# Raw-x queries in columns for the first layer-two unit of a batch, the norm's squares on DVE, 78 halves kept, and a new order

## Chip, cores and metric

The kernel runs on one core of one Trainium2 chip. The time is device microseconds per execution. The kernel before has a median of 285.7 us over 3 runs, from 284.73 to 285.88 us.

## What is computed

Two layers of decode with batch 4 and one token per batch entry, both layers with the same weights and the same caches. Each is a layer norm, attention over a cache of 4096 keys with 8 key/value heads (4 query heads on each), a residual sum, a second layer norm, a gated unit and a residual sum:

```
x = x + _A_ref(_layernorm(x, axis=-1), A_k_cache, A_v_cache, A_wq, A_wo)
x = x + _B_ref(_layernorm(x, axis=-1), B_w_gate, B_w_up, B_w_down)
x = x + _A_ref(_layernorm(x, axis=-1), A_k_cache, A_v_cache, A_wq, A_wo)
x = x + _B_ref(_layernorm(x, axis=-1), B_w_gate, B_w_up, B_w_down)
```

The caches are 32 MB each, in bf16, and do not fit on the core. Since both layers read the same cache, what is still in SBUF when layer two needs it isn't read again.

## The kernel before, in words

**Units.** The attention is cut into 16 units, written as three digits: batch entry, group of four key/value heads, layer (0 is layer one). `UNITS` names their order. A unit has four heads; K and V of a head are two *halves* each, of 512 KB (2048 keys). SBUF has a ring of 28 slots of one half each. A load fetches one half, or a *pair* (both halves of a head, 1 MB, when two neighbouring slots are free). `LOADS` is the list of all loads in the order in which SP issues them, weights between them. What `LOADS` doesn't name for a layer-two unit is *kept* from layer one: its slot stays taken until then. Counted from that table, the kernel before loads 181 halves and keeps 75 of 256, in 67 pairs and 47 single halves.

**A unit's work.** `queries` (L730) forms the unit's query from x and wq, spreads it (L767) and scales it into `zq` (L778). For each K half that comes from a load DVE transposes it in place (L805), and PE multiplies it with `zq` into the scores S (L813). `unit_probs` takes the maximum (L837 to L844), the exponential on ACT (L851), transposes the probabilities (L857, L862, L872). `unit_values` multiplies them with V (L905), ACT copies the result into a slot just read (L935, or into `p_sb`, L927), PE merges the heads (L958), and in layer one `wo` is applied and added to x (L1005, L1017).

**The chain of a batch entry.** When both layer-one units of a batch entry are done, `chain` (L1159) runs its norm (`layer_norm`, L1025, and `rstd`, L1043), gate and up products (L1069), the gated product (L1101, L1110, L1120), the down product (L1138), the sum into x (L1174) and the second norm. Only then can a layer-two query of that entry be formed: 16 matmuls that give it as rows (L743), an ACT copy (L752), 4 matmuls that turn it into columns (L757), an ACT copy (L762), the spreading (L767) and, with the inverse deviation `rs2` in the mask (L773), `zq`. The query needs x with its mean taken off (L1031).

**What sets the order.** `_Plan.schedule` (L143) takes all instructions with costs and ranks (the numbers `SHIFTS`, `CHAIN` and the like) and writes one list for each engine, gives each load its slots, and puts filler matmuls (L1380) where PE would wait. Each engine then runs its list in order. SP waits before a load until the slot's last reader is done, and every load behind it waits too.

**End.** When the last V half has landed, the rest of the last unit, the last `wo` part, the fourth norm and gated unit and the result follow (`last_part`, `last_chain`).

## Time and profile before

| | |
|---|---|
| median of 3 runs | 285.7 us (284.73 to 285.88) |
| the profiled execution | 286.48 us, of it the span of the profile 284.5 us, 1.98 us around it |
| busy | PE 227.0 us, DVE 166.5, ACT 67.6, POOL 10.7 |
| DMA | 108.8 MB through SP's queue, 94.7% of 16 engines' span |
| SP's loads | 35 V and 32 K pairs, 24 V and 23 K halves, 9 weight loads |
| granted TensorE clock | 0.946 |

Line 2 of the page cuts the span into 40 slices of 7.1 us. In the timeline of SP a row is a run of loads, from the first issue to the end of the last; a gap between rows is SP waiting for a slot. In the chain of waits "SPq L611" is SP's sequencer at a load of K or V, and a DMA row runs from an issue to its landing.

### The profile page before, as it was taken

How to read it: one execution, taken by the hardware profiler on the slowest of the kernel's cores; microseconds unless marked ns; L12 is line 12 of the kernel's file. 1: busy time of each engine (PE TensorE's matmuls, PEld its weight loads, DVE VectorE, ACT ScalarE, POOL GpSimd, SP SyncE). 2: the span in 40 equal slices, each digit the busy share in tenths (PEclk: the TensorE clock that was granted, in tenths of full speed). 3: DMA queues.
4: the chain of work that ended last, by engine and by line, in shares of the span. 5: the costliest groups of instructions: out<-in, count | busy, mean ns of one | idle time of the engine just before them, and what ended most of it. 6: DMA issues, size and time to landing. Idle time of an engine off the chain costs nothing.

```text
span 284.5 us, 7805 instructions
## 1 busy us (share of the span) xinstructions
PE 227.0 (80%) x3426; PEld 113.9 (40%) x3426; DVE 166.5 (59%) x340; ACT 67.6 (24%) x179; POOL 10.7 (4%) x39
## 2 busy tenths in 40 slices
PE   1007675669899883999989999889988898888997
PEld 1003322224455431444553444435443343534664
DVE  4537773954112493877354998304599786578222
ACT  1001002001411320231533302324232103632511
POOL 6100000000000000000000000000000000000000
PEclk9999997599799998999995999988799999999999
DMA  7999999999999999999999999998999999999910
GB/s 275 425 424 422 409 409 394 422 384 411 409 427 384 311 380 424 420 416 415 415 409 415 413 412 419 420 408 316 403 407 423 422 416 412 414 403 426 406 47 3
DMA packets 21393, 109.30 MB, mean 384 GB/s; under 512 B 2032, under 2 KB 4080, under 8 KB 12144
## 3 DMA queue, kind: packets, MB, share of 16 engines
q1 hardware_dynamic: 21296, 108.80, 94.7%
q8 instruction: 27, 0.44, 0.6%
q14 instruction: 6, 0.05, 0.0%
q10 hardware_dynamic: 64, 0.01, 0.0%
HBM read 108.79 MB, written 0.00 MB: 382 GB/s over the span
## 4 chain that ended last, share of the span: by engine, by line
PE 39%; DMA 39%; SPq 11%; DVE 7%; issue 2%; ACT 1%; DVEq 0%; ACTq 0%
DMA slots<-in_A_v_cache_dram 20%; PE S_ps L813 14%; DMA slots<-in_A_k_cache_dram 11%; SPq L611 10%; DMA wo<-in_A_wo_dram 8%; PE O_ps L905 6%; PE PT_ps L1380 4%; DVE slots L805 4%; PE M_ps L1005 3%; PE Q_ps L743 2%; PE G_ps L1140 2%; PE M_ps L958 2%; PE G_ps L1069 1%; PE U_ps L1069 1%; SPq L620 1%
## 5 line engine op out<-in xcount | busy, mean ns | idle before, releaser
L805 DVE STREAM_TRANSPOSE slots<-slots 128x1024 int32<-128x1024 int32 x87 | 103.9, 1223 | 31.1 <-DMA slots<-in_A_k_cache_dram 30.5
L813 PE MATMUL S_ps<-slots,zq 128*32 128x512 bf16 x512 | 81.0, 444 | 15.5 <-DVE slots L805 10.7
L905 PE MATMUL O_ps<-slots,pt_sb 128*16 128x512 bf16 x504 | 40.9, 410 | 10.9 <-DMA slots<-in_A_v_cache_dram 8.1
L813 PEld LDWEIGHTS S_ps<-slots,zq 128*32 128x32 bf16 x512 | 25.4, 105 | 51.9 <-DVE slots L805 17.9
L1380 PE MATMUL PT_ps<-wq 128*128 128x512 bf16 (+1 forms) x148 | 38.4, 365 | 0.7 <-ACT pt_sb L872 0.7
L935 ACT ACTIVATE slots<-O_ps 128x512 bf16<-128x512 f32 (+1 forms) x24 | 14.3, 596 | 34.5 <-PE O_ps L905 34.3
L905 PEld LDWEIGHTS O_ps<-slots,pt_sb 128*16 128x16 bf16 x504 | 11.7, 90 | 23.6 <-DMA slots<-in_A_v_cache_dram 9.0
L1380 PEld LDWEIGHTS PT_ps<-wq 128*128 128x128 bf16 x148 | 12.4, 99 | 16.1 <-issue 6.2
L872 ACT ACTIVATE pt_sb<-PT_ps 128x256 bf16<-128x256 f32 x32 | 11.0, 382 | 32.0 <-PE PT_ps L862 21.7
L851 ACT ACTIVATE p_sb<-S_ps,pt_sb 128x512 bf16<-128x512 f32 x16 | 13.3, 832 | 18.8 <-DVE pt_sb L844 16.0
L1005 PEld LDWEIGHTS M_ps<-oT,wo 128*128 128x128 bf16 x512 | 14.5, 96 | 7.9 <-issue 3.0
L1005 PE MATMUL M_ps<-oT,wo 128*128 128x32 bf16 x512 | 16.5, 177 | 0.4 <-DVE oT L980 0.4
L837 DVE TENSOR_REDUCE small<-S_ps 128x1 f32<-128x512 f32 x16 | 10.9, 684 | 9.8 <-PE S_ps L813 9.1
L712 PE MATMUL Q_ps<-small,wq 128*128 128x4 bf16 x128 | 3.7, 166 | 14.2 <-DMA wq<-in_A_wq_dram 14.2
L1057 POOL TENSOR_TENSOR stat<-real,small 128x1 f32<-128x1 f32 x8 | 4.4, 551 | 235.3 <-ACT real L1053 235.3
L958 PE MATMUL M_ps<-small,slots 128*64 128x4 bf16 (+2 forms) x196 | 9.2, 176 | 2.3 <-ACT slots L935 1.9
L958 PEld LDWEIGHTS M_ps<-small,slots 128*128 128x128 bf16 (+1 forms) x196 | 6.8, 103 | 10.1 <-ACT slots L935 5.4
L743 PE MATMUL Q_ps<-wq,small 128*1 128x512 bf16 x128 | 10.3, 387 | 0.5 <-DVE small L1031 0.4
L773 ACT ACTIVATE real<-real,stat 128x4 f32<-128x4 f32 x16 | 4.4, 293 | 25.7 <-DVE zq L778 19.8
L984 DVE TENSOR_TENSOR oT<-M_ps,real 64x8 bf16<-64x8 f32 x32 | 5.1, 159 | 8.8 <-PE M_ps L958 8.3
L927 ACT ACTIVATE p_sb<-O_ps 128x512 bf16<-128x512 f32 x8 | 4.8, 597 | 21.5 <-PE O_ps L905 17.0
L712 PEld LDWEIGHTS Q_ps<-small,wq 128*128 128x128 bf16 x128 | 3.6, 104 | 15.1 <-issue 15.1
(123 smaller groups left out, 195.6 us busy)
## 6 DMA issues: line engine op xcount, KB each, us to landing
slots<-in_A_v_cache_dram SPq DMA_DIRECT2D x35, 1024.0 KB, 10.8
slots<-in_A_k_cache_dram SPq DMA_DIRECT2D x32, 1024.0 KB, 10.3
slots<-in_A_v_cache_dram SPq DMA_DIRECT2D x24, 512.0 KB, 11.4
slots<-in_A_k_cache_dram SPq DMA_DIRECT2D x23, 512.0 KB, 8.4
wq<-in_A_wq_dram SPq DMA_DIRECT2D x2, 2048.0 KB, 14.6
wo<-in_A_wo_dram SPq DMA_DIRECT2D x4, 1024.0 KB, 19.8
wg<-in_B_w_gate_dram SPq DMA_DIRECT2D x1, 1792.0 KB, 18.3
wu<-in_B_w_up_dram SPq DMA_DIRECT2D x1, 1792.0 KB, 22.2
```

The source lines that it names most:

```text
L611: return e.dma_start(o, src)
L743: fns.append(lambda e, k=k, s=s: e.matmul(Q_ps[32 * s:32 * s + 1, :], lhsT=xT[:, b, k:k + 1], rhs=wq[:, k, hg * HC + s * 512:hg * HC + (s ...
L805: "dve", lambda e, t=t: e.transpose(ring[t.slot].bitcast(dt.int32), ring[t.slot].bitcast(dt.int32)),
L813: fns.append(lambda e, s=s, t=t, nn=nn, q=q: e.matmul(S_ps[qi][32 * s:32 * s + 32, :], lhsT=window(qi, s * NQ + nn, q), rhs=ring[t.slot].r ...
L837: dve(lambda e: e.tensor_reduce(ml[at], bank, AX.X, ALU.max, negate=True), [f"S{qi}s{s}" for s in ss], keys("ml", ss), 0.7)
L851: lambda e: e.activation(p_sb[at].rearrange("p (t j r) -> p t r j", j=32, r=2), bank.rearrange("p (t r j) -> p t r j", r=2, j=32), ACTF.Ex ...
L872: "act", lambda e, pr=pr: e.activation(pt_sb[:, (2 * i + pr) % 3], PT_ps[:, 256 * pr:256 * pr + 256], ACTF.Copy),
L905: fns.append(lambda e, m=m, at=at, v=v, c=c, q=q, pt=pt, bank=bank, x0=x0, x1=x1: e.matmul(bank[m:m + 16, x0:x1], lhsT=pt[:, at:at + 16], ...
L935: lambda e, lent=lent, rows=rows, o_ps=o_ps, rows_of=rows_of, cols=cols: e.activation(ring[lent.slot][rows, 0:cols], rows_of(o_ps[rows, 0: ...
L958: return e.matmul(o, lhsT=turned[:, tt * P + at:tt * P + at + n], rhs=heads(tt), start=(tt == 0), stop=(tt == 3))
L1005: fns.append(lambda e, k=k, n=n, h0=h0: e.matmul(M_ps[:, k * WIDE:(k + 1) * WIDE], lhsT=wo[:, h0 + n, k * P:(k + 1) * P], rhs=oT[:, b, h0 ...
L1380: return lambda e: e.matmul(PT_ps[:, column:column + width], lhsT=wq[:, 0, 0:P], rhs=wq[:, 0, 0:width], start=True, stop=True)
```

## The change

It does five things.

1. **The first layer-two query of a batch entry as columns.** `queries` has a new case `soon` (the first layer-two unit of that entry in `UNITS`): 64 matmuls of 32 columns with a 128x128 piece of wq as weights (L811 of the new kernel) give the query in columns, with no copy and no turning. The other four layer-two queries keep the 16 matmuls (L823), the copy (L832) and the turning (L837).
2. **Raw x.** All layer-two queries are formed from x itself. Two new helpers, `column_sums(0)` and `(1)`, form the negative column sums of wq once (128 matmuls at L780, two DVE copies at L789); one DVE operation (L843) adds mean times column sum to the raw query in place of the ACT copy. `rs2` no longer scales the mask, but the maximum (one more DVE operation in `unit_probs`, L935) and the exponential (its scale). The sum after the down product is written twice, first as `xT` for the query, then as x (L1282).
3. **The first norm's squares.** `layer_norm` sums x squared on DVE (L1122) beside the matmul that sums x, and `rstd` takes four times the squared mean off it on DVE (L1136, L1140, L1155) in place of three ACT operations. The second norm keeps its ACT operations (L1294, L1296) with its copy of the mean now `mean_of`.
4. **The planner.** Fillers may also go into the bank G and begin at 30 us instead of 55 us, its model of the PE clock has four phases, and its model of the DMA has 16 lanes. `SCRATCH` goes from 256 to 64 bytes.
5. **The tables.** All of them are new: the units' order, `LOADS`, `GROUPS`, the places lent to the gated unit, the ranks. Counted from the new `LOADS`, 178 halves are loaded and 78 kept, in 46 pairs and 86 single halves (31 of these are half of a head that is stored as a pair). The weights are the same nine loads.

The units before, and the core of the diff:

```
-UNITS = "000 010 100 011 110 200 001 111 210 300 211 310 101 201 311 301"
```

```diff
+UNITS = "000 010 011 100 001 110 200 111 101 210 211 300 310 201 311 301"
...
-        bus = DMA_START
+        lanes = [DMA_START] * 16
...
+            while held_wq:
+                room = fill_room(t)
+                if room is None or room[0] > at:
+                    return
+                t, reader, bank = room
+                op = _Op(len(self.ops), "pe", [self.fill(bank, FILL)], 0.2, 0.0, "pe", 1)
+                op.pairs, op.columns = 1, 4 * FILL
...
+                for since in crossed[fetches:]:
+                    lane = (fetches - 1) % 16
+                    lanes[lane] = max(lanes[lane], since) + DMA_LAG
+                    fetches += 1
+                middle = 0.0
+                for a in lanes:
+                    middle += a / 16
+                begin = op.end + DMA_DELAY
+                late = min(1.0, max(0.0, (begin - middle) / DMA_LOW + 1.0)) if middle > 20.0 else 0.0
+                lanes = [max(a, begin) + (op.size / DMA_RATE + DMA_AGAIN * late) for a in lanes]
+                op.end = max(lanes) + DMA_END + DMA_SPREAD
...
-    SCRATCH = 256
+    SCRATCH = 64
...
+    def column_sums(hg):
+        S.stage = f"c{hg}"
+        r = max(place["wq0"], place["wq1"]) + 25.0
+        for c0 in range(0, HG, 4):
+            fns = []
+            for c in range(c0, c0 + 4):
+                for k in range(KD):
+                    fns.append(lambda e, c=c, k=k: e.matmul(
+                        Q_ps[:, c * WIDE:(c + 1) * WIDE], lhsT=wq[:, k, hg * HC + c * DH:hg * HC + (c + 1) * DH],
+                        rhs=minus.broadcast_to([P, WIDE]), start=(k == 0), stop=(k == KD - 1),
+                    ))
+            S.put(
+                "pe", fns, reads=["wq0", "wq1", "Qz", "minus"], writes=[own("Q", c0 == 0)], rank=r, columns=len(fns) * 4 * WIDE,
+                lock="Q" if c0 == 0 else None,
+            )
+        S.put(
+            "dve", lambda e: e.tensor_copy(col_sum[:, hg * HG:(hg + 1) * HG], Q_ps[:, bass.ds(0, HG, step=WIDE)]),
+            reads=[own("Q")], writes=[f"cs{hg}"], cost=0.2, rank=r, free="Q",
+        )
...
+            soon = not any(u[0] == b and u[2] == 1 for u in seq[:i])
+            if soon:
+                for c0 in range(0, HG, 4):
+                    fns = []
+                    for c in range(c0, c0 + 4):
+                        for k in range(KD):
+                            fns.append(lambda e, c=c, k=k: e.matmul(
+                                Q_ps[:, c * WIDE:(c + 1) * WIDE], lhsT=wq[:, k, hg * HC + c * DH:hg * HC + (c + 1) * DH],
+                                rhs=xT[:, b, k:k + 1].broadcast_to([P, WIDE]), start=(k == 0), stop=(k == KD - 1),
+                            ))
...
+            S.put(
+                "dve",
+                lambda e, soon=soon: e.scalar_tensor_tensor(
+                    out=q2, in0=col_sum[:, hg * HG:(hg + 1) * HG], scalar=mean_of[:, b:b + 1],
+                    in1=Q_ps[:, bass.ds(0, HG, step=WIDE if soon else 1)], op0=ALU.mult, op1=ALU.add,
+                ),
+                reads=[own("Q"), f"mn{b}", f"cs{hg}"], writes=["q2"], cost=0.2, rank=rank,
             )
...
+        by, by_key = mask, "mask"
+        if l == 0:
+            by, by_key = maskrs[:, qi], f"maskrs{qi}"
+            S.put(
+                "act", lambda e: e.activation(by, mask, ACTF.Copy, scale=rs),
+                reads=["mask", rs_key], writes=[by_key], cost=0.2, rank=rank,
+            )
...
+        rs, rs_key = 1.0, []
+        if l == 1:
+            rs, rs_key = rs2[at, b:b + 1], [f"rs2{b}"]
+            dve(
+                lambda e: e.tensor_scalar(nM[at], nM[at], rs, None, op0=ALU.mult),
+                keys("nM", ss) + rs_key, keys("nM", ss), 0.16,
+            )
...
+                ACTF.Exp, bias=tr[at, 0:1], scale=rs, accum_out=ls[at],
...
+            "dve", lambda e: e.scalar_tensor_tensor(
+                out=junk, in0=x[:, b], scalar=1.0, in1=x[:, b], op0=ALU.mult, op1=ALU.mult, accum_out=xsq[:, b:b + 1]
+            ),
+            reads=[f"x{b}"], writes=["junk", f"xsq{b}"], cost=0.25, rank=rank,
...
+            "dve", lambda e: e.tensor_scalar(less, U_ps[:, 0:1], U_ps[:, 0:1], 4.0, op0=ALU.mult, op1=ALU.mult),
+            reads=["U"], writes=["less"], cost=0.16, rank=rank,
+        )
+        S.put(
+            "dve", lambda e: e.tensor_scalar(less, less, -4.0 * eps, None, op0=ALU.add),
+            writes=["less"], cost=0.16, rank=rank,
...
+            S.put(
+                "dve", lambda e: e.tensor_scalar(var[:, b:b + 1], ps_tile[:, 16:17], less, least, op0=ALU.subtract, op1=ALU.max),
+                reads=[bank, "less"], writes=["junk"], cost=0.16, rank=rank, **then,
...
+        for o, o_keys, more in ((xT, [f"xT{b}"], {}), (x, [f"x{b}", f"xsum{b}"], dict(accum_out=xsum[:, b:b + 1]))):
+            S.put(
+                "dve",
+                lambda e, o=o, more=more: e.scalar_tensor_tensor(
+                    out=o[:, b], in0=G_ps[:, bass.ds(0, KD, step=WIDE)], scalar=rs, in1=x[:, b], op0=ALU.mult, op1=ALU.add, **more
+                ),
+                reads=["G", f"rsg{b}", f"x{b}"], writes=o_keys, cost=0.2, rank=rank,
...
+        mean = mean_of[:, b:b + 1]
+        S.put(
+            "pe", lambda e: e.matmul(U_ps[:, 0:1], lhsT=ones, rhs=xsum[:, b:b + 1], start=True, stop=True),
+            reads=[f"xsum{b}", "ones"], writes=["U"], cost=0.35, rank=rank, pairs=2,
+        )
+        S.put("act", lambda e: e.activation(mean, U_ps[:, 0:1], ACTF.Copy), reads=["U"], writes=[f"mn{b}"], cost=0.18, rank=rank)
+        S.put(
+            "act", lambda e: e.activation(junk, x[:, b], ACTF.Square, bias=mean, scale=-1.0, accum_out=xsq[:, b:b + 1]),
+            reads=[f"x{b}", f"mn{b}"], writes=["junk", f"xsq{b}"], cost=0.25, rank=rank + 1.0,
+        )
...
+            for h in range(2):
+                column_sums(h)
```

**The first chain on PE.** Here are PE's rows from behind the down product (L1140, 56 matmuls, the row just ahead of these) of batch entry 0 to the scores of its first layer-two unit (011, in both kernels): L1380 is a filler, L1027 and L1049 are the second norm's, L905 and L958 values and merge of unit 010, L743 the query in rows, L757 its turning, L767 the spreading, L813 the scores. Before:

```order
L1380 MATMUL PT_ps<-wq 128x512
L1027 MATMUL U_ps<-stat 128x1
L905 MATMUL O_ps<-slots,pt_sb 16x512 x4
L743 MATMUL Q_ps<-wq,small 1x512 x8
L1049 MATMUL U_ps<-stat 128x1
L743 MATMUL Q_ps<-wq,small 1x512 x8
L905 MATMUL O_ps<-slots,pt_sb 16x512 x8
L757 MATMUL Q_ps<-small,p_sb 128x4 x4
L905 MATMUL O_ps<-slots,pt_sb 16x512 x4
L767 MATMUL Q_ps<-small,ident 32x4x4 x16
L958 MATMUL M_ps<-small,slots 128x32 x4
L813 MATMUL S_ps<-slots,zq 32x512 x32
```

After (L1247 down product, L1502 a filler, L1291 and L1150 the second norm's, L811 the query in columns, L823 the next query in rows, L852 the spreading, L901 scores, first five of unit 100, then of 011 with the next ones):

```order
L1247 MATMUL G_ps<-slots,wd 128x32 x56
L1502 MATMUL PT_ps<-wq 128x512
L811 MATMUL Q_ps<-small,wq 128x32 x16
L1291 MATMUL U_ps<-stat 128x1
L811 MATMUL Q_ps<-small,wq 128x32 x32
L1150 MATMUL U_ps<-stat 128x1
L811 MATMUL Q_ps<-small,wq 128x32 x16
L901 MATMUL S_ps<-slots,zq 32x512 x5
L852 MATMUL Q_ps<-small,ident 32x4x4 x16
L901 MATMUL S_ps<-slots,zq 32x512 x35
L823 MATMUL Q_ps<-wq,small 1x512 x16
```

The turning and its copy are gone and no V product stands in the chain any more; the scores of unit 100's first K halves now stand behind the new columns.

**SP's loads behind the weights of the gated unit.** From `wd` on, with the semaphores each load waits for (128x2048 is a half, 128x4096 a pair). Before, three loads wait only for the values of unit 000 and the fourth (K, waiting for PE, DVE and ACT) for the down product that has its slot:

```order
L620 DMA wd<-in_B_w_down_dram 128x7168
L611 DMA slots<-in_A_v_cache_dram 128x4096 [waits sem_pe]
L611 DMA slots<-in_A_v_cache_dram 128x2048 [waits sem_pe]
L611 DMA slots<-in_A_v_cache_dram 128x2048 [waits sem_pe,sem_act]
L611 DMA slots<-in_A_k_cache_dram 128x2048 [waits sem_pe,sem_dve,sem_act]
L611 DMA slots<-in_A_k_cache_dram 128x2048 [waits sem_pe] x3
L611 DMA slots<-in_A_k_cache_dram 128x2048 [waits sem_pe,sem_act]
L611 DMA slots<-in_A_k_cache_dram 128x2048 [waits sem_pe]
L611 DMA slots<-in_A_v_cache_dram 128x4096 [waits sem_pe]
L611 DMA slots<-in_A_k_cache_dram 128x4096
L611 DMA slots<-in_A_v_cache_dram 128x4096
```

After, the five loads behind `wd` wait for values of units 000 and 010, the sixth (V, waiting for PE, DVE and ACT) for the down product, the two K halves behind it for the first scores of unit 100, the pairs behind those for the scores of 011:

```order
L665 DMA wd<-in_B_w_down_dram 128x7168
L656 DMA slots<-in_A_k_cache_dram 128x2048 [waits sem_pe]
L656 DMA slots<-in_A_k_cache_dram 128x2048 [waits sem_pe,sem_act]
L656 DMA slots<-in_A_k_cache_dram 128x2048 [waits sem_pe] x2
L656 DMA slots<-in_A_v_cache_dram 128x2048 [waits sem_pe,sem_act]
L656 DMA slots<-in_A_v_cache_dram 128x2048 [waits sem_pe,sem_dve,sem_act]
L656 DMA slots<-in_A_k_cache_dram 128x2048 [waits sem_pe,sem_dve] x2
L656 DMA slots<-in_A_k_cache_dram 128x4096 [waits sem_pe] x2
L656 DMA slots<-in_A_k_cache_dram 128x4096
L656 DMA slots<-in_A_k_cache_dram 128x2048 x2
```

What stands behind `wd` without a wait for the chain went from one pair and two halves to five halves.

**SP's loads around the fourth chain.** Before, from a V pair of the last layer-one unit (310) on: four K halves of unit 201, then V pairs of 101:

```order
L611 DMA slots<-in_A_v_cache_dram 128x4096 [waits sem_pe,sem_dve]
L611 DMA slots<-in_A_k_cache_dram 128x2048 [waits sem_pe,sem_dve] x4
L611 DMA slots<-in_A_v_cache_dram 128x4096 [waits sem_pe,sem_dve]
L611 DMA slots<-in_A_v_cache_dram 128x4096 [waits sem_pe]
L611 DMA slots<-in_A_v_cache_dram 128x4096 [waits sem_dve]
L611 DMA slots<-in_A_v_cache_dram 128x2048 [waits sem_pe,sem_dve]
L611 DMA slots<-in_A_v_cache_dram 128x2048 [waits sem_dve]
L611 DMA slots<-in_A_v_cache_dram 128x2048 [waits sem_pe,sem_dve]
L611 DMA slots<-in_A_k_cache_dram 128x2048 [waits sem_dve]
```

After, from the last V pair of 310 on: nine K halves of unit 201 and 301, then V halves and K halves in turn:

```order
L656 DMA slots<-in_A_v_cache_dram 128x4096 [waits sem_pe]
L656 DMA slots<-in_A_k_cache_dram 128x2048
L656 DMA slots<-in_A_k_cache_dram 128x2048 [waits sem_pe,sem_act]
L656 DMA slots<-in_A_k_cache_dram 128x2048 [waits sem_pe]
L656 DMA slots<-in_A_k_cache_dram 128x2048
L656 DMA slots<-in_A_k_cache_dram 128x2048 [waits sem_pe]
L656 DMA slots<-in_A_k_cache_dram 128x2048 [waits sem_pe,sem_act] x2
L656 DMA slots<-in_A_k_cache_dram 128x2048 [waits sem_pe,sem_dve]
L656 DMA slots<-in_A_k_cache_dram 128x2048
L656 DMA slots<-in_A_v_cache_dram 128x4096 [waits sem_pe,sem_dve]
L656 DMA slots<-in_A_v_cache_dram 128x2048 [waits sem_pe]
L656 DMA slots<-in_A_k_cache_dram 128x2048 [waits sem_dve]
```

In the new order PE's rows around this chain are (L901 scores of 201, L1100 the `wo` product that ends 310's values, L1128 the norm's sum, L1176 gate and up, L1247 the first 24 matmuls of down; L1150 the inverse deviation, L1502 fillers):

```order
L901 MATMUL S_ps<-slots,zq 32x512 x2
L1100 MATMUL M_ps<-oT,wo 128x32 x32
L901 MATMUL S_ps<-slots,zq 32x512 x6
L1128 MATMUL U_ps<-stat 128x1
L1502 MATMUL PT_ps<-wq 128x512 x5
L1176 MATMUL G_ps<-wg,small 1x448 x8
L1150 MATMUL M_ps<-stat 128x1
L1176 MATMUL G_ps<-wg,small 1x448 x8
L1176 MATMUL U_ps<-wu,small 1x448 x16
L901 MATMUL S_ps<-slots,zq 32x512 x14
L1247 MATMUL G_ps<-slots,wd 128x32 x24
L901 MATMUL S_ps<-slots,zq 32x512 x2
```

The eighth of the nine K halves (waiting for PE and DVE) takes the slot of 201's first K half, whose scores stand on both sides of the `wo` product.

221 lines of the change are left out of this document (118 added, 103 removed).

## Prediction

> **What bounds the kernel now.** I read the page first: part 2 for the DMA row, then part 3 for the queues.
>
> ```profile
> PE   1007675669899883999989999889988898888997
> DMA  7999999999999999999999999998999999999910
> GB/s 275 425 424 422 409 409 394 422 384 411 409 427 384 311 380 424 420 416 415 415 409 415 413 412 419 420 408 316 403 407 423 422 416 412 414 403 426 406 47 3
> q1 hardware_dynamic: 21296, 108.80, 94.7%
> q8 instruction: 27, 0.44, 0.6%
> ```
>
> The DMA digit is 9 from the second slice to the 38th but once: the loads bound this kernel, while PE has slices of 5 to 7. What counts is bytes, the rate at which they flow, and the slices in which the flow is thin: the 14th (311 GB/s) and the 28th (316). I then asked for stretches by window, to have the two thin ones beside full ones.
>
> ```profile
> core 0: us, PE busy (x) PEld busy (x) DVE busy (x) ACT busy (x) POOL busy (x), PEclk, DMA share, GB/s
> 7.00:24.00 17.00, 2.13 (x80) 1.98 (x80) 7.52 (x7) 0.93 (x3) 1.29 (x3) 1.00 1.01 425
> 88.00:104.00 16.00, 14.25 (x225) 7.38 (x225) 8.57 (x19) 4.01 (x13) 0.55 (x1) 1.00 0.92 339
> 141.00:151.00 10.00, 8.84 (x176) 5.01 (x168) 4.67 (x14) 4.41 (x14) 0.90 (x2) 0.91 1.03 411
> 188.00:202.00 14.00, 12.68 (x230) 6.68 (x234) 5.25 (x14) 5.01 (x17) 1.10 (x2) 0.82 0.95 364
> 206.00:226.00 20.00, 17.17 (x226) 7.80 (x224) 17.95 (x27) 5.58 (x14) 0.00 (x0) 1.00 1.01 417
> ```
>
> 88 to 104 moved 339 x 16 = 5.42 MB; at the 411 of a full stretch that takes 13.2 us, so **2.8 us** were lost. 188 to 202 moved 5.10 MB, 12.4 us at 411: **1.6** lost. Together 4.4 us of thin flow, and no third such place. Why it is thin the timeline of SP shows (start, length, loads in a run), with the landing times of the DMA view:
>
> ```profile
> 64.65 7.10 SPq L620 DMA_DIRECT2D wd<-in_B_w_down_dram  x1
> 71.80 4.88 SPq L611 DMA_DIRECT2D slots<-in_A_v_cache_dram  x3
> 91.42 6.39 SPq L611 DMA_DIRECT2D slots<-in_A_k_cache_dram  x6
> 98.41 0.33 SPq L611 DMA_DIRECT2D slots<-in_A_v_cache_dram  x1
> wd<-in_B_w_down_dram SPq DMA_DIRECT2D x1, 1792.0 KB, 24.7
> slots<-in_A_k_cache_dram SPq DMA_DIRECT2D x1, 512.0 KB, 4.1
> ```
>
> From 76.7 to 91.4 SP issues nothing. `wd` lands at 64.65 + 24.7 = 89.35, the down product follows, and at 91.42 the half that gets its slot is issued (the second row is that half: 4.1 us to land with an emptied queue). By then only a pair and two halves were queued behind `wd`. The chain of waits has the steps:
>
> ```profile
> 80.88 0.90 PE M_ps L1005 x32
> 89.94 1.41 PE G_ps L1140 x56
> 91.36 0.24 DVE real L1174 x2
> 91.65 0.38 PE U_ps L1027 x2
> 92.03 0.53 PE O_ps L905 x4
> 94.02 0.61 ACT p_sb L752
> 94.93 0.55 PE O_ps L905 x4
> 95.50 0.61 ACT slots L935
> 96.42 1.93 PE S_ps L813 x29
> ```
>
> The end follows from the last load:
>
> ```profile
> 255.44 18.38 DMA slots<-in_A_v_cache_dram
> 273.86 0.30 PE G_ps L905 x2
> 282.43 0.27 ACT oT L1342
> ```
>
> It lands at 273.82 and 10.7 us of tail follow to the span's 284.5. So the time is (bytes at the full rate) + (thin flow) + (tail) + what lies around the span. I work against the profiled 286.48 and carry the difference to the median of 285.7, 0.8 us lower.
>
> **Part 1: the loads.** The tables go from 181 halves to 178, in 46 pairs and 86 single halves instead of 67 and 47: 39 halves more and 21 pairs fewer. What flows from 141 to 151 was issued from 132.5 to 145, and is seven single halves behind a pair; what flows from 206 to 226 was issued from 202 to 218, and is nine pairs:
>
> ```profile
> slots<-in_A_v_cache_dram SPq DMA_DIRECT2D x5, 512.0 KB, 8.1
> slots<-in_A_v_cache_dram SPq DMA_DIRECT2D x1, 1024.0 KB, 10.1
> slots<-in_A_k_cache_dram SPq DMA_DIRECT2D x2, 512.0 KB, 10.2
> slots<-in_A_k_cache_dram SPq DMA_DIRECT2D x6, 1024.0 KB, 8.4
> slots<-in_A_v_cache_dram SPq DMA_DIRECT2D x3, 1024.0 KB, 10.6
> ```
>
> A half is 0.524 MB: 1.276 us at 411. A pair is 1.049 MB: 2.515 at 417, or 2.467 at the 425 of 7 to 24 us. 39 x 1.276 = 49.8; 21 pairs are 52.8 or 51.8. The change is -3.0 or -2.0; I take the middle, **-2.5**. So splitting costs next to nothing in a full queue. Instructions are loaded too: 27 packets for 7805 instructions in the rows above, one per 289. The new program has about 650 more (324 matmuls, each counted with its weight load): 2.3 packets more, 0.6% of 284.5 us over 27 is 0.06 us of all 16 engines each, 1 us for one engine if it takes them alone. I take **+0.2**.
>
> The Trainium skill, page "DMA: Bandwidth & Descriptors", section "Bandwidth", speaks against this part: it asks for transfers of 1 MiB or more to reach 75% of a peak that it gives as 435 GB/s. By it a half runs at no more than some 327 GB/s, 1.60 us, an estimate from that page; 39 of them less 21 pairs of 2.515 would be +9.6 in the place of -2.5. The 411 above disagrees for a filled queue; the 339 of 88 to 104, where each half waits by itself, agrees. Its mechanism is rival C below.
>
> **Part 2: the thin flow.** What is thin afterwards depends on how much SP may issue behind `wd` before the chain releases more. I set a rule on the stretch of before: the supply is all loads ahead of the first late one, and lateness is that load's landing less the supply. Its first late half: 91.42 + 4.1 - 89.35 = 6.2; supply 2.515 + 2 x 1.276 = 5.1; late 1.1. Five more halves follow one by one at 16 us / (5.42 / 0.524 = 10.3 halves) = 1.55 each, 0.27 over the full rate: 1.1 + 1.4 = 2.5, against 2.8 measured. The rule serves.
>
> First chain, after. Five halves are free of the chain; the sixth takes the down product's slot, which comes as before 2.1 us after `wd` has landed, with 5 x 1.276 = 6.4 us of supply against 6.2: not late. The seventh and eighth wait for scores of unit 100, and the pairs behind for scores of 011. These scores now stand directly behind the columns: 0.6 + 1.41 (down product) + 0.24 (sum) + the columns + 0.76 (two norm matmul rows of 0.38, L1027 above) + 1.1 to 1.8 (16 to 27 scores at the 1.93 / 29 of the last chain row) + 0.3 to the issue. The columns are 64 matmuls of 32 columns; the trace has them at 0.90 for 32 (L1005) and 1.41 for 56 (L1140): 1.6 to 1.8. Sum 6.0 to 6.9, landing 10.1 to 11.0, supply of seven halves 8.9: late by 1.2 to 2.1. The V product and the two ACT copies of 0.61 (L752, L935) that stood in the old path are gone; what is late next are the pairs behind the scores of 011, for nothing up to 1.7 us (half of the old stretch's five late loads, 1.4, and the unknown of one PE row more). Range 1.2 to 3.8. I take **1.6**, near the lower end, because PE goes through those scores in one row of 35.
>
> Second chain: eighteen single halves in a row, all released by values and scores, not by the query. The nearest row is 141 to 151, a run of halves at 411 with no loss: 0; the far bound is three late ones at 0.27, 0.8. I take **0.4**. Third chain: only one load waits for its down product, behind pairs: 0, as in 141 to 151.
>
> Fourth chain: seven K halves ahead of the eighth, which waits for the first scores of 201; these stand on both sides of the `wo` product (0.90), so it is late by nothing up to that. Behind the eighth, a V pair and V halves wait for more scores, among them 14 that stand behind the norm and gate and up. The old first stretch's G and U products and their norm are these rows:
>
> ```profile
> 84.14 0.40 PE U_ps L1027 x2
> 84.93 0.74 PE G_ps L1069 x12
> 85.98 0.29 PE G_ps L1069 x4
> 86.27 0.76 PE U_ps L1069 x16
> ```
>
> From 84.14 to 87.03 that is 2.9 us, of which a pair's 2.515 covers most. Bounds 0.5 to 2.6 (the 188 to 202 stretch, in which the same engines wait, lost 1.6). I take that row's **1.5**. Sum after: 1.6 + 0.4 + 0 + 1.5 = 3.5, between 1.7 and 7.2. Against 4.4: **-0.9**.
>
> **Part 3: engines.** Column sums: 128 matmuls, 128 x 0.028 (L1005) = 3.6 us of PE, in slices 4 to 8 where PE's digits are 5 to 7, and two DVE copies. The DVE operations of the first norm, the maximum and the query add some 20 of about 0.15:
>
> ```profile
> L1017 DVE SCALAR_TENSOR_TENSOR real<-M_ps,real 128x4 f32<-128x4 f32 x16 | 2.4, 153 | 7.9 <-PE M_ps L1005 7.8
> L773 ACT ACTIVATE real<-real,stat 128x4 f32<-128x4 f32 x16 | 4.4, 293 | 25.7 <-DVE zq L778 19.8 <-POOL stat L702 5.4 <-POOL stat L1057 0.5
> ```
>
> 20 x 0.153 = 3 us of DVE's 284.5, where it is busy 166.5; half of the sixteen 0.293 us ACT operations go. All of it lies under the loads: nothing. If that cover went, four chains with four more DVE steps of 0.15 would cost 2.4. The maximum's extra step is 0.15 in each layer-two unit; it is on the path only where the last unit's probabilities wait, and the tail behind the last landing (10.7 us) holds values, merge, `wo` and the gated unit, which stand in the same order: 0, within 0.3.
>
> **Sum**: -2.5 + 0.2 - 0.9 = -3.2: the profiled execution to 283.3, the median to **282.5**.
>
> **Rivals.** T = 285.7 - 2.3 + (S - 4.4), S the thin flow.
>
> A, no thin flow is left (S = 0): the new order holds every load far enough ahead. For it: every full stretch above shows single halves without loss; against it: 6.0 us of path behind `wd` are longer than the old 2.1. 279.0.
>
> B, no change: all bounds at their upper ends, S = 7.2. For it: the pairs behind 011 and the V loads of the fourth chain are new waits in the place of the removed ones. 286.2.
>
> C, slower: the half-by-half flow of 88 to 104 (0.27 lost per half) becomes the rule in the run of 18 halves at the second chain and in 22 of the loads from the fourth chain's K halves on, because each slot comes free singly and no pair refills the queue. 40 x 0.27 = 10.8, with 1.6 of the first chain S = 12.4: 291.4. It makes the kernel slower from S = 8.1 on, that is from 24 such halves. For it: it is what happened twice before; against it: 141 to 151, seven halves in a row at 411.
>
> **How the numbers follow.** Forecast 0.50, A 0.16, B 0.14, C 0.20. I leave out C. The range then goes from A less half a microsecond of the pair's rate, 278.5, to B with 1.3 for that rate and the instruction packets, **287.5**. A change of under 0.5%, 284.3 to 287.1, is about what a measurement of this kernel cannot tell from none. Forecast and A are faster (0.66), B the same (0.14), C slower (0.20).
>
> **What would show it.** Part 1: full stretches with single halves at 405 GB/s or more; at 330 part 1 is wrong. Part 2: the slice behind `wd`'s landing at over 360 instead of 311 GB/s, and a gap of SP before the seventh load there; a thin slice of under 330 near the fourth chain, or a run of halves around the second one below 390, would be B or C. The last half should land some 3.2 us before 273.8, with the 10.7 us behind it unchanged; a longer tail would mean that one of the engine edits is not hidden.

## The result, and the profile after

The changed kernel takes 289.0 us in the median (286.15 to 290.41, 6 runs) beside 285.65 for the kernel before: 1.0112 of it, with an interval of 1.0079 to 1.0146. Measured once more among the experiments it took 287.35 us, 1.0061 (1.0025 to 1.0096). It is slower, by 1.7 to 3.3 us. Forecast was 282.5, so faster, with a range up to 287.5: the first measurement lies outside it, the second just inside. The first profiled execution took 290.41 us with a span of 288.4.

The page of after, parts 2 and 3:

```profile
PE   1000696787888979998989968988977978889996
DMA  6999999999999999999999999999999998799900
GB/s 249 424 398 419 414 400 407 390 416 402 417 367 295 415 421 422 410 415 420 409 411 361 338 418 415 418 418 414 417 411 423 418 409 305 287 323 401 415 32 3
q1 hardware_dynamic: 23888, 107.23, 93.6%
```

The thin slice behind `wd` is still there (295 GB/s in the 13th), a shallow one is new (361 and 338 in the 22nd and 23rd), and where before had two thin slices, after has three in a row near the end (305, 287, 323). The windows of after around these places, and one full stretch:

```profile
core 0: us, PE busy (x) PEld busy (x) DVE busy (x) ACT busy (x) POOL busy (x), PEclk, DMA share, GB/s
84.00:100.00 16.00, 14.16 (x179) 6.28 (x176) 13.11 (x21) 2.97 (x7) 0.55 (x1) 1.00 0.93 342
152.00:168.00 16.00, 13.71 (x330) 8.74 (x325) 9.39 (x23) 3.32 (x9) 1.10 (x2) 1.00 0.98 355
184.00:204.00 20.00, 17.52 (x305) 9.37 (x303) 10.63 (x32) 4.83 (x10) 0.55 (x1) 1.00 1.02 416
238.00:262.00 24.00, 20.76 (x356) 11.18 (x358) 18.63 (x44) 4.76 (x13) 1.10 (x2) 0.93 0.87 314
```

Read as in the prediction, against 411 GB/s: the first loses 16 x (1 - 342/411) = 2.7 us, the second 2.2, the last 24 x (1 - 314/411) = 5.7. Together **10.6 us of thin flow**. The kernel before had 4.4, and 3.5 were forecast for this one. In the second profile of after (span 285.0) the same windows move 342, 383 and 329 GB/s: 2.7 + 1.1 + 4.8 = 8.6.

The last stretch in SP's timeline of after (nine K halves of units 201 and 301, then V and K loads in turn), and the chain of waits beside it:

```profile
220.87 22.04 SPq L656 DMA_DIRECT2D slots<-in_A_k_cache_dram  x9
246.47 1.63 SPq L656 DMA_DIRECT2D slots<-in_A_v_cache_dram  x2
248.15 0.49 SPq L656 DMA_DIRECT2D slots<-in_A_k_cache_dram  x1
248.76 0.37 SPq L656 DMA_DIRECT2D slots<-in_A_v_cache_dram  x1
253.52 0.80 SPq L656 DMA_DIRECT2D slots<-in_A_k_cache_dram  x2
```

```profile
225.30 13.35 DMA slots<-in_A_k_cache_dram
238.68 1.25 DVE slots L893
239.98 0.39 PE S_ps L901 x2
240.37 0.90 PE M_ps L1100 x32
241.27 0.76 PE S_ps L901 x6
242.02 0.31 PE U_ps L1128 x2
...
245.46 1.16 PE S_ps L901 x12
...
276.03 1.04 PE M_ps L1310 x32
...
286.29 0.27 ACT oT L1459
```

The DMA view of after, with the time from issue to landing, for the loads issued at 53.88 (`wd`), 242.11 and 246.47:

```profile
wd<-in_B_w_down_dram SPq DMA_DIRECT2D x1, 1792.0 KB, 26.2
slots<-in_A_k_cache_dram SPq DMA_DIRECT2D x1, 512.0 KB, 4.1
slots<-in_A_v_cache_dram SPq DMA_DIRECT2D x1, 1024.0 KB, 6.4
```

Three places are to be seen. The K half issued at 225.30 lands at 238.65; DVE turns it until 239.93, PE multiplies it, and only when its scores end at 242.03 is the slot free that the eighth of the nine K halves takes (issued at 242.11). The V pair at 246.47 is issued when the row of scores that begins at 245.46 is nearly done. And the last V half, issued at 266.13 with 10.4 us to landing, lands at 276.5, 2.7 us later than in before; behind it stand 11.9 us to the span's end instead of 10.7, since PE is then still at the `wo` product of 276.03, which ends at 277.07 (11.0 us in the second profile).

### The profile page after: what moved, and what is told of

Read it like the earlier page. It is cut to its first block, busy times and chain, and to the rows that moved or that the text cites. A ratio compares the mean times of both kernels' runs of the same rounds, so it can differ in the third digit from the quotient of the medians.

```text
span 288.4 us, 8429 instructions
## 1 busy us (share of the span) xinstructions
PE 223.9 (78%) x3714; PEld 118.5 (41%) x3750; DVE 171.4 (59%) x377; ACT 60.4 (21%) x143; POOL 10.7 (4%) x40
## 4 chain that ended last, share of the span: by engine, by line
DMA 35%; PE 34%; SPq 19%; DVE 7%; issue 3%; ACT 1%; ACTq 0%
DMA slots<-in_A_k_cache_dram 22%; SPq L656 16%; PE S_ps L901 12%; DMA wd<-in_B_w_down_dram 9%; PE O_ps L1000 5%; DMA slots<-in_A_v_cache_dram 4%; DVE slots L893 4%; PE G_ps L1247 3%; SPq L665 2%; PE Q_ps L811 2%; PE PT_ps L1502 2%; PE M_ps L1053 1%; PE M_ps L1310 1%; PE M_ps L1100 1%; PE G_ps L1176 1%
## 5 line engine op out<-in xcount | busy, mean ns | idle before, releaser
L901 PE MATMUL S_ps<-slots,zq 128*32 128x512 bf16 x512 | 73.1, 418 | 10.3 <-DVE slots L893 5.4
L1000 PE MATMUL O_ps<-slots,pt_sb 128*16 128x512 bf16 x504 | 39.9, 395 | 10.1 <-DMA slots<-in_A_v_cache_dram 8.2
L901 PEld LDWEIGHTS S_ps<-slots,zq 128*32 128x32 bf16 x512 | 24.0, 101 | 43.7 <-DVE slots L893 8.6
L1502 PE MATMUL PT_ps<-wq 128*128 128x512 bf16 (+1 forms) x110 | 30.8, 370 | 2.8 <-issue 2.2
L757 PE MATMUL Q_ps<-small,wq 128*128 128x4 bf16 x128 | 3.6, 165 | 23.8 <-DMA wq<-in_A_wq_dram 23.8
L1502 PEld LDWEIGHTS PT_ps<-wq 128*128 128x128 bf16 x140 | 11.5, 99 | 15.6 <-issue 8.8
L1100 PE MATMUL M_ps<-oT,wo 128*128 128x32 bf16 x512 | 15.6, 176 | 2.7 <-issue 1.6
L1100 PEld LDWEIGHTS M_ps<-oT,wo 128*128 128x128 bf16 x512 | 13.9, 96 | 8.0 <-issue 2.3
L757 PEld LDWEIGHTS Q_ps<-small,wq 128*128 128x128 bf16 x128 | 3.5, 101 | 23.8 <-DMA wq<-in_A_wq_dram 23.8
L1112 DVE SCALAR_TENSOR_TENSOR real<-M_ps,real 128x4 f32<-128x4 f32 x16 | 2.6, 162 | 15.2 <-PE M_ps L1100 15.2
L866 DVE TENSOR_TENSOR zq<-Q_ps,real 128x256 bf16<-128x256 f32 x16 | 6.5, 404 | 7.0 <-PE Q_ps L852 6.9
L1208 ACT ACTIVATE slots<-G_ps,stat 128x192 f32<-128x192 f32 (+2 forms) x11 | 4.7, 435 | 25.7 <-POOL stat L1164 16.4
L946 ACT ACTIVATE p_sb<-S_ps,pt_sb 128x512 bf16<-128x512 f32 x8 | 6.6, 830 | 14.6 <-DVE pt_sb L939 13.9
L946 ACT ACTIVATE p_sb<-S_ps,pt_sb,stat 128x512 bf16<-128x512 f32 x8 | 7.5, 933 | 10.6 <-PE Q_ps L823 5.2
## 6 DMA issues: line engine op xcount, KB each, us to landing
slots<-in_A_v_cache_dram SPq DMA_DIRECT2D x44, 512.0 KB, 10.7
```

The costliest lines, as they stand in the source:

```text
L901: fns.append(lambda e, s=s, t=t, nn=nn, q=q: e.matmul(S_ps[qi][32 * s:32 * s + 32, :], lhsT=window(qi, s * NQ + nn, q), rhs=ring[t.slot].r ...
L946: lambda e: e.activation(p_sb[at].rearrange("p (t j r) -> p t r j", j=32, r=2), bank.rearrange("p (t r j) -> p t r j", r=2, j=32), ACTF.Ex ...
L1000: fns.append(lambda e, m=m, at=at, v=v, c=c, q=q, pt=pt, bank=bank, x0=x0, x1=x1: e.matmul(bank[m:m + 16, x0:x1], lhsT=pt[:, at:at + 16], ...
L1100: fns.append(lambda e, k=k, n=n, h0=h0: e.matmul(M_ps[:, k * WIDE:(k + 1) * WIDE], lhsT=wo[:, h0 + n, k * P:(k + 1) * P], rhs=oT[:, b, h0 ...
L1502: return lambda e: e.matmul(ps_of[:, 0:width], lhsT=wq[:, 0, 0:P], rhs=wq[:, 0, 0:width], start=True, stop=True)
```

## The experiments

Most runs take something out of a kernel *behind* its planner, so that the order on every engine, the slots and the loads stay as they were: the instructions for which a condition holds are dropped, and whoever waited for one waits for what that one had waited for.

```diff
+        gone = [op for op in self.ops if CONDITION]
+        for op in gone:
+            for u in self.ops:
+                if op in u.deps:
+                    u.deps.discard(op)
+                    u.deps |= {d for d in op.deps if not (d.eng == u.eng == "pe")}
+            self.prog[op.eng].remove(op)
+            self.ops.remove(op)
```

Line numbers of these kernels are up to 8 higher than in after. Ratios are to the kernel before on the same chip. Three theories follow one another: Theory 1, that the fourth chain's products stand on the path to the end and that transfers ahead of the last layer-one V count one for one; a second, here the rival in the runs on DVE's steps, that the change's own steps lengthen the chains; and Theory 3, a loop over slots.

| run | what it is | median us | ratio | interval |
|---|---|---|---|---|
| first result | after | 289.0 | 1.0112 | 1.0079 to 1.0146 |
| after_again | after | 287.35 | 1.0061 | 1.0025 to 1.0096 |
| dma_before | loads of before alone | 271.64 | 0.9526 | 0.9470 to 0.9582 |
| dma_after | loads of after alone | 270.16 | 0.9473 | 0.9417 to 0.9529 |
| thin_after | after, late V loads halved | 286.33 | 1.0046 | 1.0012 to 1.0079 |
| early_after | after, V loads of 210 halved | 282.52 | 0.9908 | 0.9866 to 0.9950 |
| thin_before | before, late V loads halved | 283.1 | 0.9935 | 0.9905 to 0.9965 |
| early_before | before, V loads of 210 halved | 282.27 | 0.9911 | 0.9869 to 0.9952 |
| no4_after | after, no products in chain 4 | 286.43 | 1.0040 | 1.0005 to 1.0075 |
| no4_before | before, the same | 285.95 | 1.0014 | 0.9974 to 1.0055 |
| no1_after | after, no products in chain 1 | 286.79 | 1.0036 | 0.9997 to 1.0075 |
| no2_after | after, no products in chain 2 | 287.37 | 1.0065 | 1.0031 to 1.0100 |
| nodve_after | after, 16 DVE steps fewer | 286.44 | 1.0059 | 1.0023 to 1.0095 |
| dve_before | before, 16 DVE steps more | 285.3 | 0.9999 | 0.9962 to 1.0036 |
| notr_after | after, 8 transposes of 201 fewer | 285.5 | 1.0012 | 0.9984 to 1.0040 |
| notr4_after | both notr and no4 | 284.06 | 0.9965 | 0.9939 to 0.9992 |

### The loads alone

The work between the loads and the output is replaced by one column's copy for each load:

```diff
+    for t in tiles.values():
+        S.put("dve", lambda e, t=t: e.tensor_copy(real[:, 0:1], ring[t.slot][:, 0:1]), tiles=(t,), writes=["junk"], cost=0.1)
```

Expected of dma_before: 

> All attention and layer work is left out: the loads of before in their order, each slot released by a copy of one column on DVE. Both theories: about 273 us (the last load of before lands at 273.8 us, 4.4 us of that were thin flow; some 2 us behind it and 2 us around the span). It is the floor of before's bytes.

Expected of dma_after: 

> The same for the loads of after. Theory 1 (what is lost is lost in waits and at the end of the fourth chain, the split itself costs nothing): 2 to 3 us below dma_before. Rival (39 halves more in single loads cost the stream): above dma_before, by up to 9 us.

dma_before is 1.4 us below the 273 expected, and after's loads are done 1.5 us earlier (270.16 against 271.64), less than the 2 to 3 expected. From 30 to 260 us the first moves 416 GB/s and the second 414, though it has 86 single halves in the place of 47:

```profile
30.00:260.00 230.00, 24.91 (x162) 0.00 (x0) 1.00 1.02 416
```

```profile
30.00:260.00 230.00, 25.06 (x163) 0.00 (x0) 1.00 1.02 414
```

The rival in its form (after's loads slower, by up to 9 us) is out. But the split isn't free: the three halves fewer are 1.57 MB, 3.8 us at 416 GB/s, and only 1.5 us are saved. Some 2 us go to the split and the new order of the loads, which these runs don't tell apart. Of the forecast 2.3 us of Part 1, 1.5 are there. The last landings in these two runs, from the chains of dma_before and dma_after, are 266.09 and 264.44:

```profile
244.88 21.21 DMA slots<-in_A_v_cache_dram
```

```profile
247.97 16.47 DMA slots<-in_A_v_cache_dram
```

So before's last load (273.82) is 7.7 us behind its floor, and after's (276.5) 12.0.

### Late transfers and early ones

V loads of the named units fetch half of their bytes, the rest of the values is stale; the plan is the same.

```diff
+            if kind == "v" and u in THIN:
+                return e.dma_start(o[:, 0:len(qs) * TH * DH // 2], src[:, 0:len(qs) * TH * DH // 2])
             return e.dma_start(o, src)
```

Expected of thin_after: 

> After, with the V loads of units 201 and 301 fetching half of their bytes (15 halves, about 9.6 us of transfer less; the other half of these values is stale). Theory 1 (from the fourth chain on, the engines' own chain sets the end): 0 to 1.5 us below after's 289.0. Rival (the stream still sets the end): 5 us or more below.

Expected of early_after: 

> After, with the V loads of unit 210 fetching half of their bytes (8 halves, 5.1 us of transfer less, ahead of the last V load of layer one). Theory 1 (the landing of unit 310's V plus some 50 us of engine work sets the end): 4 to 5 us below after's 289.0, so more than the 2 us that 9.6 us of late transfer gave. Rival (the stream sets the end, the late run was only caught by the next limit): about the same as the late run per us of transfer, 1 to 2 us below.

Expected of thin_before: 

> Before, with the V loads of units 201 and 301 fetching half of their bytes (15 halves, 9.6 us). Theory 1: in before the stream sets the end and the engines stand 3 to 5 us behind it, so 3 to 5 us below 285, more than in after. Rival: as in after, 1 to 2 us below.

Expected of early_before: 

> Before, with the V loads of unit 210 fetching half of their bytes (8 halves, 5.1 us). Both theories: 4 to 5 us below 285; if it is much less, transfers do not add to the time one for one even in before.

In after, 9.6 us of transfer less at the end give 0.4 to 1.9 us (from 1.0061 or 1.0112 to 1.0046), and 5.1 us less ahead of the last layer-one V give 4.4 to 5.8: early bytes count one for one, late ones hardly. This is as Theory 1 has it. For before it missed twice: the late 9.6 us give 1.9, not 3 to 5, and the early 5.1 us give 2.5, not 4 to 5. So in both kernels something other than the late bytes keeps the time from falling by more than 2 us; what it is, these runs don't show. That time lost early isn't made up later shows in after, and in before only for half of it.

### Without the products of a chain

```diff
+        gone = [op for op in self.ops if op.stage in ("g3", "h3", "d3") and op.columns + (op.stage == "h3") and op.eng in ("pe", "act", "dve")]
```

The same with 0 and 1 for the first and second chain. Left out are gate, up, the gated product and down of that chain; the norms stay.

Expected of no4_after: 

> After, with the gate, up, gated and down products of the fourth chain left out behind the planner, the order of everything else kept. Theory 1: these steps and a filler stand on the path that sets the end (2.0 us gate and up, 1.7 us down, 1.0 us of a filler, the gated product between them): 4 to 6 us below after's 289.0. Rival: 0 to 1 us below.

Expected of no4_before: 

> Before, with the gate, up, gated and down products of the fourth chain left out behind the planner. Theory 1: the fourth chain of before stands beside the stream, 0 to 1 us below 285. Rival (the engines' chain bounds before as well): 2 us below, as in after.

Expected of no1_after: 

> After, with the gate, up, gated and down products of the first chain left out behind the planner, the order of the rest kept. Theory 1 (thin flow ahead of the last layer-one V counts one for one): 2 to 3 us below after's 289, the thin flow behind wd's landing. Rival (only what stands behind the last layer-one V counts, the first chain is made up later): 0 to 1 us below.

Expected of no2_after: 

> After, with the same products of the second chain left out. Theory 1: the halves behind the second chain flow thinly (2 us by the trace) because PE works on the chain while their slots wait for values and scores: 1.5 to 2.5 us below after's 289. Rival (single halves flow thinly by themselves): no change, 0 to 0.5 us.

Without the fourth chain's products after gains 0.6 to 2.1 us, far from the 4 to 6 expected, and before nothing. Without the second chain's it gains 1.3 us against the first measurement and nothing against the second. Without the first's, 0.7 to 2.2, so that Theory 1 (2 to 3) and its rival (0 to 1) both stay possible. SP in no1_after, DVE and PE beside it, and a window with the granted clock:

```profile
80.38 0.33 SPq L664 DMA_DIRECT2D slots<-in_A_v_cache_dram  x1
85.25 5.92 SPq L664 DMA_DIRECT2D slots<-in_A_k_cache_dram  x6
```

```profile
81.54 2.54 DVE L901 STREAM_TRANSPOSE slots<-slots 128x1024 int32<-128x1024 int32 x2 [0.72 <-DMA slots<-in_A_k_cache_dram]
```

```profile
80.61 0.61 PE L819 MATMUL Q_ps<-small,wq 128*128 128x32 bf16 x16 [2.82 <-DVE small L1290]
83.29 1.46 PE L909 MATMUL S_ps<-slots,zq 128*32 128x512 bf16 x3
82.00:86.00 4.00, 4.00 (x60) 2.36 (x57) 3.51 (x5) 0.43 (x3) 0.55 (x1) 0.50 0.91 362
```

and the same in after:

```profile
81.82 0.33 SPq L656 DMA_DIRECT2D slots<-in_A_v_cache_dram  x1
85.36 6.44 SPq L656 DMA_DIRECT2D slots<-in_A_k_cache_dram  x7
82.17 2.37 DVE L893 STREAM_TRANSPOSE slots<-slots 128x1024 int32<-128x1024 int32 x2
82.05 0.57 PE L811 MATMUL Q_ps<-small,wq 128*128 128x32 bf16 x16 [0.32 <-DVE small L1282]
84.23 0.83 PE L901 MATMUL S_ps<-slots,zq 128*32 128x512 bf16 x3
82.00:86.00 4.00, 3.95 (x92) 2.98 (x92) 3.98 (x7) 0.73 (x4) 0.55 (x1) 1.00 0.91 359
```

With the down product gone, the load that takes its slot is issued 1.44 us earlier, but the next one only 0.11 us earlier. Its slot is that of a K half of unit 100, which lands at 81.5 in no1_after and at 81.3 in after. DVE has turned it by 82.8 and by 83.4; PE comes to its four scores at 83.29 and at 84.23, in both runs behind the query's columns, which begin when the chain's sum is done (80.61 and 82.05). So this load stands behind the chain too. The 1.44 us that it could gain are lost on PE: the granted clock from 82 to 86 us is 0.50 in no1_after and 1.00 in after, and from the first column to the end of the four scores pass 4.6 us instead of 3.2. Whether the chain's products cause the first thin stretch is therefore not decided by this run. no2_after has the same flaw:

```profile
152.00:168.00 16.00, 13.18 (x203) 6.38 (x206) 7.56 (x16) 1.93 (x6) 1.10 (x2) 0.68 0.95 362
```

A clock of 0.68 stands there against the 1.00 of after's window above. What the times do refute is Theory 1's main claim, that the fourth chain's products are worth 4 to 6 us.

### The change's own steps on DVE

```diff
+        gone = [op for op in self.ops if op.eng == "dve" and ((op.keys == {"less"}) or any({"junk", "xsq%d" % b} <= op.keys for b in range(4)) or (op.cost == 0.16 and any(k.startswith("rs2") for k in op.keys)))]
```

takes 16 of them out of after; into before the same number goes, as products of a constant into cells that nobody reads:

```diff
+        for op in self.ops:
+            if op.eng == "dve" and ((op.stage[:1] == "n" and any(k.startswith("xT") for k in op.keys)) or (op.cost == 0.22 and op.stage in ["p%d" % i for i in LATE])):
+                op.fns = [self.idle() for _ in range(2 if op.stage[:1] == "n" else 1)] + op.fns
```

Expected of nodve_after: 

> After without 16 of the DVE steps that the change added: x squared and the constant of the first norm (4 each) and the maximum's inverse deviation (8). The result is off by these factors, the order of the rest is the same. Theory 1 (the new order loses the time, the steps lie beside other work): 0 to 0.7 us below after's 289. Rival (the code edits lengthen the chains): 1.5 us or more below.

Expected of after_again: 

> The changed kernel itself once more, as the base of the runs that took parts of it away (their gains of 1.3 to 2.2 us are near the width of one interval). Both theories: 1.008 to 1.014 of before. If it is 1.006 or less, the gains without the second chain (1.0065) and without the DVE steps (1.0059) are none.

Expected of dve_before: 

> Before with 16 more DVE steps of 128x4 at the places where the change put its own (two ahead of each first norm's x without mean, one ahead of each layer-two maximum's turn), order and loads as before. Theory 1 (the order loses the time, the steps themselves lie beside other work): within 0.3% of before. Rival (the steps lengthen the chains whatever the order): 1 us or more above before.

nodve_after seemed to gain 1.5 us against the first 1.0112; against 1.0061 it gains nothing, and 16 steps more in before cost nothing (0.9999). The rival is out to about 0.4%: the steps lie beside other work in before, and no cost of theirs shows in after. What the query in columns is worth by itself was not tried.

### The loop over slots

```diff
+        gone = [op for op in self.ops if op.eng == "dve" and op.stage in ("k13.0", "k13.1")]
```

for notr_after (the scores of unit 201 are then made of K halves that are not turned); notr4_after has this and no4's condition.

Expected of notr_after: 

> After, with the eight DVE transposes of unit 201's K halves left out (its scores are wrong), all orders kept. Theory 3 (in the fourth stretch each late load waits for a K half of 201 that landed only five or six halves earlier: landing, transpose, scores, release, issue and transfer are a loop longer than that): the loop is 1.2 to 3 us shorter, the thin flow from 240 to 262 falls from about 5 to 2 to 3 us, and the time 1.5 to 2.5 us from 1.006 to 1.008 of before, to 0.998 to 1.002. Rival (the chain's norm, gate and up rows that stand ahead of the scores in PE's queue hold them): 0 to 0.7 us.

Expected of notr4_after: 

> After without those eight transposes and without the fourth chain's gate, up, gated and down products. Theory 3: what the transposes give comes here too, and the chain's products add 1 us or more, since with the loop shortened PE's rows ahead of the scores are next: 3 us or more below after, 0.990 to 0.996 of before. Rival (the products alone): as without the products alone, 1.004.

The transposes alone give 1.4 to 2.9 us, to 1.0012, inside what Theory 3 expected. With the products gone as well it is 0.9965, just outside the expected 0.990 to 0.996, and below before. The window 238 to 262 us of no4_after, notr_after and notr4_after, in this order:

```profile
238.00:262.00 24.00, 20.01 (x317) 10.21 (x316) 18.54 (x44) 5.37 (x14) 1.10 (x2) 0.93 0.86 325
```

```profile
238.00:262.00 24.00, 22.07 (x434) 12.40 (x435) 12.76 (x42) 6.33 (x16) 1.10 (x2) 1.00 0.94 353
```

```profile
238.00:262.00 24.00, 21.30 (x381) 11.35 (x377) 12.69 (x43) 6.09 (x16) 1.10 (x2) 1.00 0.99 384
```

325, 353 and 384 GB/s are 5.0, 3.4 and 1.6 us of thin flow, against 4.8 to 5.7 in after: the products alone move it by at most 0.7, the transposes by 1.4 or more (Theory 3 expected 2 to 3 us to be left, and 3.4 are), both together by 3.2 or more. SP's V pair says more. Its row in no4_after, notr_after and notr4_after:

```profile
246.43 1.53 SPq L664 DMA_DIRECT2D slots<-in_A_v_cache_dram  x2
```

```profile
243.94 1.67 SPq L664 DMA_DIRECT2D slots<-in_A_v_cache_dram  x2
```

```profile
241.94 1.56 SPq L664 DMA_DIRECT2D slots<-in_A_v_cache_dram  x2
```

Without the products it comes when it came in after (246.47); without the transposes 2.5 us earlier; without both, 4.5. Part of that was gained ahead of it: the later of the two K halves whose slots it takes lands at 242.4 in after, and at 242.8, 240.7 and 240.7 in these three. From that landing to the issue of the pair pass **4.1 us in after, 3.6 without the products, 3.3 without the transposes and 1.3 without both**. So the slot hangs on two things at once: the K half has to be turned, and its scores stand in PE's row behind the norm, gate and up. Taking away one leaves the other. They aren't quite independent, since DVE does the transposes and the norm in one row: in after its first step behind the norm's matmul (L1132, 242.83) comes 0.5 us after that matmul's end, behind a transpose that began at 241.67, and in notr_after the same step (239.93) comes at once. So the runs show that landing, transposes, norm, products and scores together hold the slot; how much of it is the loop and how much the chain, they don't. Nor do the times show that the products count more once the transposes are gone: 1.3 us then (1.0012 to 0.9965), 0.6 to 2.1 alone. In no4_after the granted clock fell to 0.50 from 244.4 to 247.6 us, which may hide a few tenths of what the products cost.

## Why the prediction was wrong

**What held.** With the thin flow as measured, 8.6 or 10.6 us, the formula of the prediction, 285.7 - 2.3 + (S - 4.4), gives 287.6 or 289.6; measured are 287.35 and 289.0. So most of the miss lies in S. That it comes so near is in part luck: the 2.3 were 1.5, and the tail, taken as unchanged, is longer. In profiled executions the floor is 266.09 - 264.44 = 1.65 us lower, the last load 12.0 instead of 7.7 us above it, the tail 1.2 us longer: -1.65 + 4.3 + 1.2 = 3.9, the 288.4 - 284.5 of the spans. That this comes out is arithmetic and proves nothing; it says where the time is. The third chain cost nothing, as forecast (its down product is at 202.4 us, and the 29th to 31st slices, 202 to 224 us, have 417, 411 and 423 GB/s), and the change's DVE steps cost nothing that shows.

**The step that failed** is Part 2, the fourth chain: "seven K halves ahead of the eighth, which waits for the first scores of 201 ... so it is late by nothing up to that [0.9]", with 1.5 us for the whole stretch, at most 2.6. It measured 4.8 to 5.7. The supply was counted from a wrong beginning. The eighth load's slot belongs to the second of those same seven K halves (the one issued at 225.30; not to 201's first, as the text on the loads around this chain has it). So not seven halves flow while it waits but the five in between, 5 x 1.276 = 6.4 us, and what it waits for begins only with the landing of that second half: 238.65 to the issue at 242.11 is 3.5 us (transpose, scores, the `wo` product between them), and 4.1 more to its landing. That is 1.2 us more than the supply; the last section shows that this half lands at the pace of the one ahead all the same, while the flow around it is thin. The larger loss is the V pair behind it, whose wait for the scores behind norm, gate and up the prediction held to be mostly covered. It has four halves in between, 5.1 us, and a path of 4.1 us from the landing of its K half (242.4) to 246.47 and 6.4 to its own landing: 10.5 us, where the four halves and the pair itself need 7.6. **This one load loses 2.9 us.**

The rule that served for the stretch of before, all loads ahead of the first late one, served there because the wait was for `wd`, which lies ahead of all of them. It also counts the late load's own transfer as lost: before's half of 91.42 lands at 95.5, 1.2 us behind the one ahead of it (94.3), and the rule calls it 1.1 late. That it gave 2.5 for the measured 2.8 was partly luck.

**The first chain**, 1.6 forecast, 2.7 measured, failed by the same count. The path was right: the sixth load came 1.7 us behind `wd`'s landing (53.88 + 26.2 = 80.1) for 2.1 forecast, the eighth (86.33) 6.2 for 6.0 to 6.9. But I took the seventh as supply. It waits for scores of unit 100 as well, is issued only at 85.36 and is itself late. **The second chain**, 0.4 forecast and at most 0.8, is 1.1 to 2.2; what holds its halves is not shown. **The tail**, 0 within 0.3, is 0.3 to 1.2 longer. The prediction named a longer tail as a sign of an engine edit that isn't hidden; here PE's `wo` product stands across the last landing, and no run separates the new order from the edits there.

**Part 1**, -2.3 forecast, is -1.5: right in sign; single halves flow at nearly the rate of pairs (414 beside 416 GB/s), but the loads save less than their bytes.

**Rival C** has the sign and, with 291.4, a time not far off, and its point of decision (8.1 us of thin flow) was passed. Its mechanism is not what happened: dma_after streams the same single halves at 414 GB/s. By the Trainium skill, page "DMA: Bandwidth & Descriptors", section "Bandwidth", it takes transfers of 1 MiB or more to reach 75% of the peak. The 414 of dma_after disagrees for a queue that is kept filled. So do the 342 and 355 GB/s of two of the stretches with waits above, and before's 339, which the prediction took as agreeing: all lie over the 327 that it estimated from the page. Only the 314 of the last stretch is below.

**What stays open**: why after's runs spread from 285.5 to 290.4 us, and how much of the 78 kept halves, which hold slots until the fourth chain, is in the short loops. No run had more slots, and the first and the second chain were never without their products at the clock of after.

## What to carry to other kernels

For each load of a ring of buffers, find the load whose data must be used before its slot is free, and count only the bytes between those two as supply; if landing, use, release, issue and transfer take longer than these bytes, the stream thins, however long the list of loads ahead looks. In after, bytes saved behind such a point bought little (0.4 to 1.9 us for 9.6) and bytes saved ahead of it bought themselves (4.4 to 5.8 for 5.1); in before the early ones bought half (2.5). A cause isn't refuted by a run that takes it away while a second one holds the same slot. And a run that takes work off PE needs its granted clock read beside it: here it was half of the clock it was compared with.

## What the runs showed of the hardware

In these traces a load counts as landed at the last of 16 signs, taken here as one from each of the 16 DMA engines. In the trace of after the last sign was 0.6 us behind the mean of the 16 at the first loads and 2.6 us at the K half that lands at 238.65; in the loads of after alone it grew from 0.5 to 1.7, while the stream moved 414 GB/s. At the eighth K half of the last stretch the distance falls from 2.4 us (the half ahead, landing at 244.88) to 0.75 (246.16). So by the last sign this half comes 1.3 us behind the one ahead, at the full pace, and by the mean 2.9 us behind it: most engines had nothing to move there (the DMA share from 242 to 243 us is 0.27), and the thin flow in GB/s shows that where the landings don't yet. The profile lists the program's own instructions among the packets of these engines:

```profile
q8 instruction: 29, 0.48, 0.7%
```

29 packets in after, most of them 1.0 to 1.1 us long. The distance rises from 1.5 to 2.6 us between the landings at 229.9 and 233.6, and one such packet begins at 231.3. In the loads of after alone, which have no q8 packets, it rises from 0.8 to 1.7 between 179.0 and 182.5, and one of the three instruction packets that another queue has in that time of loading begins at 179.2. That such packets cause the steps fits this; no run tried it.
